# Linear attention and gated MLP on one core: another table of order, normalization as multiply-add, a tail by batch halves, more filler matmuls

## The chip, the core and the metric

The kernel runs on one core of a Trainium2 chip. The metric is the device time of one execution in microseconds (us). The engines are TensorE (PE, its weight loads PEld), VectorE (DVE), ScalarE (ACT), GpSimd (POOL) and SyncE (SP, which here only issues DMAs). Each engine takes its instructions strictly in the order in which the program lists them and waits on semaphores for the others.

## The reference

Linear attention with exponential features, then a feed-forward block with a spatial gate. B = 8 batches, H = 8 heads, S = 576 tokens, D = 64, F = 128, model width 512, inner width 1024.

```python
def phi(x):
    proj = np.einsum('bhsd,df->bhsf', x, w_phi)
    proj = proj - np.max(np.abs(proj), axis=-1, keepdims=True)
    return np.concatenate([np.exp(proj), np.exp(-proj)], axis=-1)
q_p, k_p = phi(q), phi(k)
kv = np.einsum('bhsf,bhsd->bhfd', k_p, v)
z = np.sum(k_p, axis=2)
num = np.einsum('bhsf,bhfd->bhsd', q_p, kv)
den = np.einsum('bhsf,bhf->bhs', q_p, z)[..., None] + 1e-06
x = (num / den)                       # then heads side by side: (B, S, 512)
h = np.maximum(x @ w_in, 0.0)
u, v = h[..., :512], h[..., 512:]
v_n = (v - mean(v)) / np.sqrt(var(v) + 1e-06)
v_s = np.einsum('ts,bsd->btd', w_spatial, v_n) + b_spatial[None, :, None]
out = (u * v_s) @ w_out
```

## The kernel before

**Tiling.** The 576 tokens of a batch are 512 in four chunks of 128, and a tail of 64. The tails of two batches make one tile of 128 rows; such a pair of batches is a group `g` (four groups). Most steps exist in a main form and in a form for tails, with a `t` in its name.

**The table of order.** The body of the kernel is a list of words, `ORDER`, which is read from left to right; each word calls one small function that issues the instructions of one step, and nothing reorders them. So the table sets the order on every engine and in every DMA queue. A word such as `qp.1.0.1:1,4` is the step `qp` for batch 1, half 0, head group 1, with its output in PSUM banks 1 and 4; `@A`, `@V`, `@P`, `@S` choose the engine where there is a choice; in other words the number behind the colon is a buffer of the step's kind of tile.

**The steps, keys.** `lk` loads a batch of k (POOL's queue, with a cast), `xk` turns it by a DMA transpose (SP's queue), `kp` projects it into two PSUM banks (8 matmuls, line 517), `km` takes the largest absolute value (VectorE, 522), `ke` makes the two exponentials (ScalarE, 526), `kem` those of the maxima, `vs` scales v by these on POOL (575), `kv` multiplies the two (606, 608), `kvc` copies the product out.

**Queries.** `lq`, `xq`, `qp`, `qm` correspond; `qs` splits the maxima into two bf16 parts (POOL, 623 and 624), `qt` transposes them, `qc` copies, `qf` makes the transposed projection less the maxima in two banks (633, 637), `qe` the exponentials (642), `qn` numerator and denominator (689), `qr` and `qx` the quotient (695, 702). `xx` turns the result by a DMA transpose, `tx` and `txc` do the same on TensorE.

**Feed-forward.** `vm` (798) and `um` (880) are the two halves of the first product, `vr` and `ur` their rectifiers, `vb` and `va` mean and variance, `vx` adds epsilon (VectorE, 803), `vw` takes the power -0.5 (POOL, 806), `vn` normalizes (POOL, 809), `sm` is the spatial product (895, 897), `sg` the gate (904), `om` the last product (909), `oc` its copy, `od` the store. `warm` issues matmuls of the identity into a bank that nobody reads. `lin`, `lout`, `lsp`, `lspt`, `lbs` load the weights, `spt`, `spc`, `spb` prepare the spatial ones.

**PSUM.** All eight banks are one tile of 128 x 8 x 512 f32. A step with one bank uses `bank(i)`; a step with two uses a slice with a step between its two banks:

```python
def pair(i, j):
    return ps[:, bass.ds(i, 2, step=j - i), :]
```

The waits between engines are put in when the program is built, from the tiles and slices that instructions read and write. Steps with two banks are `kp`, `km`, `ke`, `qp`, `qm`, `qf`, `qe`, `qn`, `qr`, `qx` and their tail forms.

Of the kernel before, what the change touches and what calls it, by code (L numbers as in the profile page):

```python
# [17 lines left out]
zvst.0@V lkf.0:0,0@S lkf.1:1@S lkf.2:2@S lq0.0.4:1 lkf.3:3@S lphi.0@A lphi.1@A lq0.4.4 lv.0.1:0@A zsp@V zmhl.0@V  # L18
lk.1:2 cident lv.0.0:1@A cphi@V zvnt.1@A ckf.1@A ckf.2@P lkt.0:0@S ckf.0@V warm.2:7 tk.0.0.0:0 csel tkc.0.0.0:0@V
warm.3:7 kp.0.0:1,2 tk.0.0.1:3 warm.10:7 tk.0.1.0:4 tkc.0.0.1@A chalf@P zmhl.1@V csel2@V km.0.0:0 ke.0.0.0:0 zmhl.2@V  # L20
ckf.3@P kem.0.0:0 kp.0.1:5,6 ke.0.0.1 lqt.0:1@S xq.0.0:1 lvt.0:0@S tkc.0.1.0:2@V xq.0.1:3 warm.3:3 kp.0.2:0,7 km.0.1:1
lv.2.0:2@S tk.0.1.1:3 ke.0.1.0:1 tkc.0.1.1@V km.0.2:2 ckt.0:0@P tkt.0:4 tktc.0:0@V kp.0.3:1,3 kem.0.1:1 kpt.0:2,4
ke.0.1.1 lq.1:0 vs.0.0.0:0@P km.0.3:3 kmt.0:0 qp.0.0.0:5,6 ke.0.2.0:2 ke.0.2.1 kemt.0:2 qm.0.0.0:0 qp.0.1.0:0,7
kem.0.3:3 qm.0.1.0:1 xk.1.0:4 ke.0.3.0:3 qs.0.0.0:0@V qp.0.0.1:5,6 lin.0 ket.0.0:0 ke.0.3.1 qs.0.1.0:1@V vs.0.0.1@P
vs.0.1.0:1@P qt.0.1.0:0 qt.0.0.0:7 cqt.0:0@V qp.0.1.1:1,3 qc.0.1.0:0@A qc.0.0.0:1@A qm.0.0.1:2 ket.0.1 vst.0.0.0:0@P
# [125 lines left out]
def kernel(  # L151
# [16 lines left out]
    nc = tc.nc  # L168
# [836 lines left out]
```

## Time and profile before

| | us |
|---|---|
| three timed runs | 452.3, 453.0, 456.23 (median 453.0) |
| the profiled execution | 445.4 |
| its span, first to last instruction | 443.6 |
| PE / PEld busy | 290.5 / 171.9 |
| DVE / ACT / POOL busy | 221.6 / 195.2 / 216.0 |
| mean granted TensorE clock | 0.807 |

Times in a profile are counted from the first instruction of the program. "Busy" is the time in which an engine had an instruction under way; of TensorE the ends are modelled, and the clock that was granted to it is shown beside. A group's row gives line, engine, operation, tiles and shapes, count, busy time and mean ns of one, then the idle time just before these instructions and what ended it. DMA moved 44.1 MB, at about 200 GB/s in the first 55 us and 99 GB/s over the span.

### The profile page before, as it was taken

What the parts mean: (1) busy time and instruction counts of PE and PEld (TensorE: products, weight loads), DVE (VectorE), ACT (ScalarE), POOL (GpSimd) and SP (SyncE); (2) the same over time, 40 slices, a digit from 0 to 9 for tenths busy, and PEclk for the clock granted to TensorE, in tenths of its full rate; (3) what the DMA queues carried; (4) which work ended last, traced back from release to release, by engine and by line L of the source; (5) the groups of instructions that cost most, each with busy time, mean ns of one, the idle gap of its engine ahead of it and who ended that gap; (6) DMA issues with size and microseconds to landing.
All of it is one profiled execution on the core that took longest, in us unless ns stands there. A gap on an engine that the chain in (4) does not pass through costs nothing. (4 is left out here: it accounts for less than half of the span.)

```text
span 443.6 us, 7949 instructions
## 1 busy us (share of the span) xinstructions
PE 290.5 (65%) x3184; PEld 171.9 (39%) x3184; DVE 221.6 (50%) x411; ACT 195.2 (44%) x314; POOL 216.0 (49%) x280
## 2 busy tenths in 40 slices
PE   4246463555765446554765668687879767699996
PEld 3125322224444233322333344344535535444452
DVE  5463424434853343332334358647778643666452
ACT  4254334344853433243242456375776555113032
POOL 3552241235674292501098029195579695446600
PEclk9556655666966766666677869999999999999999
DMA  8999965150980633936044748174233115012245
GB/s 198 203 225 222 191 121 99 20 72 0 148 151 2 143 49 47 193 46 142 1 62 82 110 69 160 33 190 113 33 84 72 51 24 120 2 25 83 60 142 191
DMA packets 91065, 44.11 MB, mean 99 GB/s; under 512 B 59986, under 2 KB 86290, under 8 KB 91028
## 3 DMA queue, kind: packets, MB, share of 16 engines
q1 hardware_dynamic: 72388, 32.39, 33.7%
q0 software_dynamic: 17424, 10.10, 17.7%
q10 hardware_dynamic: 1216, 1.11, 0.8%
q8 instruction: 25, 0.41, 0.4%
q14 instruction: 12, 0.10, 0.1%
HBM read 32.85 MB, written 9.44 MB: 95 GB/s over the span
## 5 line engine op out<-in xcount | busy, mean ns | idle before, releaser
L642 ACT ACTIVATE qf<-banks 128x1024 bf16<-128x1024 f32 x72 | 71.9, 1024 | 79.8 <-PE banks L880 11.9
L575 POOL TENSOR_TENSOR vs<-v,em 128x512 bf16<-128x512 f32 x62 | 64.1, 1041 | 87.5 <-ACT em L532 66.5
L526 ACT ACTIVATE kf<-banks 128x1024 bf16<-128x1024 f32 x64 | 65.1, 1027 | 64.6 <-DVE mk L522 20.4
L522 DVE TENSOR_REDUCE mq<-banks 128x8 f32<-128x1024 f32 x36 | 43.9, 1220 | 47.7 <-PE banks L608 9.6
L809 POOL TENSOR_SCALAR vn<-vr,mv,rs 128x512 bf16<-128x512 bf16 x30 | 62.1, 2073 | 1.1
L522 DVE TENSOR_REDUCE mk<-banks 128x8 f32<-128x1024 f32 x36 | 43.8, 1220 | 29.3 <-PE banks L608 9.4
L517 PE MATMUL banks<-wphi,T 64*128 64x128 bf16 x512 | 32.3, 262 | 37.6 <-ACT kf L526 11.2
L798 PE MATMUL banks<-w_in,xT 128*128 128x512 bf16 x128 | 40.0, 446 | 13.6 <-DVE x L702 4.2
L806 POOL TENSOR_TENSOR rs<-mv,neghalf 128x2 f32<-128x2 f32 (+1 forms) x20 | 13.7, 684 | 66.1 <-DVE mv L803 62.1
L895 PE MATMUL banks<-w_spT,vn 128*128 128x512 bf16 x128 | 36.3, 410 | 7.9 <-ACT kf L526 4.3
L517 PEld LDWEIGHTS <-T 64*128 64x128 bf16 x512 | 21.3, 112 | 51.8 <-issue 43.9
L606 PE MATMUL banks<-vs,kf 128*128 128x66 bf16 x512 | 30.4, 215 | 15.1 <-ACT qf L642 4.8
L880 PE MATMUL banks<-xT,w_in 128*128 128x512 bf16 x128 | 35.8, 415 | 2.4 <-ACT ob L253 1.5
L606 PEld LDWEIGHTS <-kf 128*128 128x128 bf16 x512 | 27.6, 112 | 23.0 <-issue 10.5
L909 PE MATMUL banks<-w_out,uT 128*128 128x512 bf16 x128 | 33.8, 401 | 3.4 <-DVE x L702 2.0
L689 PE MATMUL banks<-kv,qf 128*128 128x66 bf16 x512 | 25.6, 209 | 12.1 <-ACT qf L642 4.8
L689 PEld LDWEIGHTS <-qf 128*128 128x128 bf16 x512 | 23.7, 109 | 21.5 <-issue 17.8
L904 DVE TENSOR_TENSOR uT<-banks,uT 128x512 bf16<-128x512 f32 x32 | 21.5, 683 | 20.3 <-PE banks L897 11.5
L702 DVE TENSOR_TENSOR x<-banks,rc 128x512 bf16<-128x512 f32 x32 | 22.1, 690 | 17.3 <-PE banks L517 5.7
L253 ACT COPY ob<-banks 128x512 f32<-128x512 f32 x23 | 13.2, 587 | 38.5 <-PE banks L909 24.0
L608 PE MATMUL banks<-vst,kft 128*128 128x66 bf16 x128 | 25.4, 214 | 0.0
L798 PEld LDWEIGHTS <-xT 128*128 128x128 bf16 x128 | 12.7, 107 | 29.2 <-issue 19.6
(117 smaller groups left out, 466.5 us busy)
## 6 DMA issues: line engine op xcount, KB each, us to landing
out_dram<-ob SPq DMA_DIRECT2D x32, 256.0 KB, 2.7
v<-in_v_dram SPq DMA_DIRECT2D x14, 512.0 KB, 4.8
ld<-in_k_dram POOLq DMA_DIRECT2D x7, 512.0 KB, 7.9
ld<-in_q_dram POOLq DMA_DIRECT2D x7, 512.0 KB, 6.8
ob<-in_k_dram SPq DMA_DIRECT2D x4, 256.0 KB, 3.1
v<-in_v_dram ACTq DMA_DIRECT2D x2, 512.0 KB, 12.8
tf<-in_k_dram SPq DMA_DIRECT2D x8, 128.0 KB, 5.1
tf<-in_q_dram SPq DMA_DIRECT2D x8, 128.0 KB, 5.9
```

The costliest lines, as they stand in the source:

```text
L517: nc.tensor.matmul(out=bank(banks[y])[:, n * F:(n + 1) * F], lhsT=xT[halves[y], n, :], rhs=wphi[halves[y], :], start=True, stop=True)
L522: nc.vector.tensor_reduce(out=out_, in_=pp.rearrange("p y (n f) -> p y n f", f=F), axis=AX.X, op=ALU.max, apply_absolute_value=True)
L526: nc.scalar.activation(out=kf[:, s].rearrange("p y n f -> p y (n f)"), in_=pp, func=AF.Exp, bias=0.0, scale=(1.0, -1.0)[s])
L575: ENG[e].tensor_tensor(out=at["vs", (b, j)][:, s, :, 0:D], in0=at["v", (b, j // 2)][:, (j % 2) * n:(j % 2 + 1) * n, :], in1=at["em", (b, j ...
L606: nc.tensor.matmul(out=pv[:, hh, s, :], lhsT=kf[:, s, c % 2, 2 * hh + c // 2, :], rhs=w[:, s, NB * hh + c, :], start=(c == 0), stop=False)
L642: nc.scalar.activation(out=at["qf", u][:, s].rearrange("p y n t -> p y (n t)"), in_=at["pq", u], func=AF.Exp, bias=0.0, scale=(1.0, -1.0)[s])
L689: nc.tensor.matmul(out=at["pn", u][:, y, n, :], lhsT=f[:, s, y, n, :], rhs=at["kv", b][:, hg * HH + n, s, :], start=(s == 0), stop=(s == 1))
L798: nc.tensor.matmul(out=bank(place), lhsT=lhs[:, kc, :], rhs=w_in[:, kc, HALF:DFF], start=(kc == 0), stop=(kc == KC - 1))
L809: ENG[e].tensor_scalar(out=out_, in0=in_, scalar1=mv, scalar2=rs, op0=ALU.subtract, op1=ALU.mult)
L880: nc.tensor.matmul(out=bank(place).rearrange("p (c t) -> p c t", c=NB), lhsT=w_in[:, kc, dc * P:(dc + 1) * P], rhs=at["xT", b][:, :, kc, : ...
L895: nc.tensor.matmul(out=bank(place), lhsT=at["vn", b][:, c, cs], rhs=w_spT[:, c, 0:T0], start=(c == 0), stop=False)
L909: nc.tensor.matmul(out=bank(place), lhsT=at["uT", b][:, dc, c * P:(c + 1) * P], rhs=w_out[:, dc, :], start=(dc == 0), stop=(dc == KC - 1))
```

## The change

Nothing of the buffers changes. What changes:

- **Normalization.** `vn` and `vnt` compute x * rs + m rather than (x - mean) * rs. `vx` (now `prepare`) adds epsilon to the variance and negates the mean, in two instructions; the new steps `vy` and `vyt` multiply the negated mean by `rs` on POOL, behind `vw`.
- **Tails.** The steps behind a tail's features (`qnt` to `vnt`) take a part: 0 or 1 for one batch of the group, 2 for both. Group 0 is run in two parts, groups 1 to 3 whole. Group 0's parts are turned on TensorE (`txt`, `txtc`), group 3 as before, groups 1 and 2 by DMA as before.
- **Loads.** The loads of tails are written by one helper with the same two DMAs. `lphi` is one DMA on SP's queue rather than two on ACT's. `lk`, `lq` and `lv` are unchanged.
- **Fillers.** `warm` writes the last quarter of a bank. There are 117 of its matmuls in 12 words rather than 18 in four: 25, 10, 9, 12, 7, 5, 2, 20, 7, 12, 4 and 4, all ahead of `qt.0.1.0`.
- **The table.** All of `ORDER` is new: other places, other banks and buffers, and other engines for some copies and rectifiers (`vr` 23 on ACT and 9 on VectorE, before 14 and 18; `txc` 6 and 2, before 2 and 6). The feed-forward steps of batch 0 stand right behind its attention; `lsp`, `lspt`, `lin` and `lout` are issued earlier, `lq.1`, `lk.2`, `lq.2` later.

The first words of the old and of the new table, and the place in each where the feed-forward block of batch 0 begins:

```diff
-zvst.0@V lkf.0:0,0@S lkf.1:1@S lkf.2:2@S lq0.0.4:1 lkf.3:3@S lphi.0@A lphi.1@A lq0.4.4 lv.0.1:0@A zsp@V zmhl.0@V
-lk.1:2 cident lv.0.0:1@A cphi@V zvnt.1@A ckf.1@A ckf.2@P lkt.0:0@S ckf.0@V warm.2:7 tk.0.0.0:0 csel tkc.0.0.0:0@V
...
-qr.0.1.1:0 txc.0.1@V kem.1.1:1 qp.1.0.0:2,5 ke.1.0.1 ke.1.1.0:0 kem.1.0:3 kp.1.2:0,7 lbs:0@S qx.0.1.1 qtt.0:1 vm.0.0:3
-qm.1.0.0:1 qp.1.1.0:2,5 vs.1.1.0:0@P vst.0.1.1@P qct.0:0@V vm.0.1:1 km.1.2:3 ke.1.1.1 vr.0.0:0@A ke.1.2.0:1 tx.0.2:4
...
+zsp@V zmhl.1@V zmhl.0@V zmhl.2@V cident lkf.0:0,0@S csel zvnt.1@A lkf.2:1@S zvnt.0@A lphi@S ckf.0@V warm.25:0
+tk.0.0.0:0 lkf.1:2@S lkt.0:0@S lkf.3:3@S lq0.0.4:1 ckf.2@V tkc.0.0.0:0@A warm.10:0 tk.0.1.0:1 lv.0.0:0@A cphi@V
...
+vbt.0.0:0 qr.0.1.1:1 txc.0.1@V vat.0.0:0 vst.0.1.1@P vm.0.0:4 vxt.0.0 qx.0.1.1 spc.4@A vm.0.1:6 vr.0.0:1@V ckt.1:0@P
+lv.1.1:3@S tx.0.2:3 vwt.0.0:0 vb.0.0:1 tx.0.3:2 lq.2:1 vr.0.1:2@A spt.3:0 kp.1.0:1,7 kp.1.1:4,5 txc.0.3@A vyt.0.0
...
```

The functions:

```diff
...
         return bass.AP(tensor=t.tensor, offset=t.offset + (b * H + h0) * S * D,
                        ap=[[NB * D, P], [S * D, n], [1, NB * D]])
 
-    def tail_ap(t, b):
-        return bass.AP(tensor=t.tensor, offset=t.offset + b * H * S * D + T0 * D,
-                       ap=[[D, TL], [S * D, H], [1, D]])
-
-    rows = [slice(0, TL), slice(TL, 2 * TL)]
+    def load_tail(e, out_, t, g):
+        for bl in range(2):
+            ENG[e].dma_start(out=out_[bl * TL:(bl + 1) * TL],
+                             in_=bass.AP(tensor=t.tensor, offset=t.offset + (2 * g + bl) * H * S * D + T0 * D,
+                                         ap=[[D, TL], [S * D, H], [1, D]]))
+
+    rows = [slice(0, TL), slice(TL, 2 * TL), slice(0, P)]
+    parts = [(0,), (1,), (0, 1)]
     halves = [slice(0, D), slice(D, P)]
     ops = {}
 
...
         make_identity(nc, ident)
 
     @op
-    def lphi(e, i):
-        ENG[e].dma_start(out=wphi_f[i * D:(i + 1) * D, :], in_=w_phi)
+    def lphi(e):
+        ENG[e].dma_start(out=wphi_f, in_=bass.AP(tensor=w_phi.tensor, offset=w_phi.offset, ap=[[0, 2], [F, D], [1, F]]))
 
     @op
     def cphi(e):
...
     @op
     def warm(e, n, place):
         for i in range(n):
-            nc.tensor.matmul(out=bank(place)[:, 0:F], lhsT=ident, rhs=ident, start=True, stop=True)
+            nc.tensor.matmul(out=bank(place)[:, 3 * P:4 * P], lhsT=ident, rhs=ident, start=True, stop=True)
 
 
 
...
 
     @op
     def lkt(e, g, place):
-        t = take("tf", ("k", g), place)
-        for i in range(2):
-            ENG[e].dma_start(out=t[rows[i]], in_=tail_ap(k, 2 * g + i))
+        load_tail(e, take("tf", ("k", g), place), k, g)
 
     @op
     def lqt(e, g, place):
-        t = take("tf", ("q", g), place)
-        for i in range(2):
-            ENG[e].dma_start(out=t[rows[i]], in_=tail_ap(q, 2 * g + i))
+        load_tail(e, take("tf", ("q", g), place), q, g)
 
     @op
     def ckt(e, g, place):
...
 
     @op
     def lvt(e, g, place):
-        t = take("vt", g, place)
-        for i in range(2):
-            ENG[e].dma_start(out=t[rows[i]], in_=tail_ap(v, 2 * g + i))
+        load_tail(e, take("vt", g, place), v, g)
 
     @op
     def lin(e, i):
...
         query_exp(g, s)
 
     @op
-    def qnt(e, g, p0, p1):
-        at["pn", g] = sums((p0, p1))
+    def qnt(e, g, i, p0, p1):
+        at["pn", g, i] = sums((p0, p1))
         for y in range(2):
             for n in range(HH):
                 for s in range(2):
-                    for bl in range(2):
+                    for bl in parts[i]:
                         r = rows[bl]
-                        nc.tensor.matmul(out=at["pn", g][r, y, n, :], lhsT=at["qf", g][:, s, y, n, r],
+                        nc.tensor.matmul(out=at["pn", g, i][r, y, n, :], lhsT=at["qf", g][:, s, y, n, r],
                                          rhs=at["kv", 2 * g + bl][:, 2 * n + y, s, :], start=(s == 0), stop=(s == 1))
 
     @op
-    def qrt(e, g, place):
-        nc.vector.reciprocal(out=take("rc", g, place), in_=at["pn", g][:, :, :, D:D + 1])
-
-    @op
-    def qxt(e, g, place):
-        nc.vector.tensor_tensor(out=take("xt", g, place).rearrange("p (n y) d -> p y n d", y=2),
-                                in0=at["pn", g][:, :, :, 0:D], in1=at["rc", g].to_broadcast([P, 2, HH, D]),
-                                op=ALU.mult)
+    def qrt(e, g, i, place):
+        nc.vector.reciprocal(out=take("rc", (g, i), place)[rows[i]], in_=at["pn", g, i][rows[i], :, :, D:D + 1])
+
+    @op
+    def qxt(e, g, i, place=None):
+        if place is not None:
+            take("xt", g, place)
+        r = rows[i]
+        nc.vector.tensor_tensor(out=at["xt", g].rearrange("p (n y) d -> p y n d", y=2)[r],
+                                in0=at["pn", g, i][r, :, :, 0:D],
+                                in1=at["rc", (g, i)][r].to_broadcast([r.stop - r.start, 2, HH, D]), op=ALU.mult)
 
 
 
...
         nc.sync.dma_start_transpose(out=take("xTt", g, place), in_=at["xt", g].rearrange("p h d -> p (h d)"))
 
     @op
-    def txt(e, g, place):
+    def txt(e, g, i, place):
         pt = bank_bf(place)[:, 0:KC * P].rearrange("p (n t) -> p n t", t=P)
+        r = rows[i]
         for kc in range(KC):
-            nc.tensor.transpose(out=pt[:, kc, :], in_=at["xt", g][:, 2 * kc:2 * kc + 2, :], identity=ident)
-        at["px", g] = pt
-
-    @op
-    def txtc(e, g, place):
-        copy(e, take("xTt", g, place), at["px", g])
-
-
-
-    def v_mm(lhs, place):
+            nc.tensor.transpose(out=pt[:, kc, r], in_=at["xt", g][r, 2 * kc:2 * kc + 2, :], identity=ident[r, r])
+        at["px", g, i] = pt[:, :, r]
+
+    @op
+    def txtc(e, g, i, place=None):
+        if place is not None:
+            take("xTt", g, place)
+        copy(e, at["xTt", g][:, :, rows[i]], at["px", g, i])
+
+
+
+    def v_mm(lhs, place, r=slice(0, P)):
         for kc in range(KC):
-            nc.tensor.matmul(out=bank(place), lhsT=lhs[:, kc, :], rhs=w_in[:, kc, HALF:DFF], start=(kc == 0),
+            nc.tensor.matmul(out=bank(place)[r], lhsT=lhs[:, kc, r], rhs=w_in[:, kc, HALF:DFF], start=(kc == 0),
                              stop=(kc == KC - 1))
-        return bank(place)
-
-    def add_eps(mv):
-        nc.vector.tensor_scalar(out=mv, in0=mv, scalar1=1e-6, scalar2=None, op0=ALU.add)
-
-    def root(rs, mv):
-        nc.gpsimd.tensor_tensor(out=rs, in0=mv, in1=neghalf[:, 0:rs.shape[1]], op=ALU.pow)
+        return bank(place)[r]
+
+    def prepare(mv):
+        nc.vector.tensor_scalar(out=mv[:, :, 1], in0=mv[:, :, 1], scalar1=1e-6, scalar2=None, op0=ALU.add)
+        nc.vector.tensor_scalar(out=mv[:, :, 0], in0=mv[:, :, 0], scalar1=-1.0, scalar2=None, op0=ALU.mult)
+
+    def root(rs, mv, r=slice(0, P)):
+        nc.gpsimd.tensor_tensor(out=rs, in0=mv, in1=neghalf[r, 0:rs.shape[1]], op=ALU.pow)
+
+    def shift(mv, rs):
+        nc.gpsimd.tensor_tensor(out=mv, in0=mv, in1=rs, op=ALU.mult)
 
     def normalize(e, out_, in_, mv, rs):
-        ENG[e].tensor_scalar(out=out_, in0=in_, scalar1=mv, scalar2=rs, op0=ALU.subtract, op1=ALU.mult)
+        ENG[e].tensor_scalar(out=out_, in0=in_, scalar1=rs, scalar2=mv, op0=ALU.mult, op1=ALU.add)
 
     @op
     def vm(e, b, c, place):
...
 
     @op
     def vx(e, b, cc):
-        add_eps(at["mv", (b, cc)][:, :, 1])
+        prepare(at["mv", (b, cc)])
 
     @op
     def vw(e, b, cc, place):
         root(take("rs", (b, cc), place).rearrange("p n o -> p (n o)"), at["mv", (b, cc)][:, :, 1])
+
+    @op
+    def vy(e, b, cc):
+        shift(at["mv", (b, cc)][:, :, 0], at["rs", (b, cc)][:, :, 0])
 
     @op
     def vn(e, b, c, place=None):
...
         normalize(e, at["vn", b][:, c, 0:HALF], at["vr", (b, c)], at["mv", (b, cc)][:, y, 0:1], at["rs", (b, cc)][:, y, :])
 
     @op
-    def vmt(e, g, place):
-        at["pV", g] = v_mm(at["xTt", g], place)
-
-    @op
-    def vrt(e, g, place):
-        relu(e, take("vr", g, place), at["pV", g])
-
-    @op
-    def vbt(e, g, place):
-        nc.vector.bn_stats(out=take("st", g, place), in_=at["vr", g])
-
-    @op
-    def vat(e, g, place):
-        nc.vector.bn_aggr(out=take("mv", g, place)[:, 0, :], in_=at["st", g])
-
-    @op
-    def vxt(e, g):
-        add_eps(at["mv", g][:, 0, 1:2])
-
-    @op
-    def vwt(e, g, place):
-        root(take("rs", g, place)[:, 0, :], at["mv", g][:, 0, 1:2])
-
-    @op
-    def vnt(e, g, place):
-        t = take("vnt", g, place)
-        for bl in range(2):
+    def vmt(e, g, i, place):
+        at["pV", g, i] = v_mm(at["xTt", g], place, rows[i])
+
+    @op
+    def vrt(e, g, i, place):
+        relu(e, take("vr", (g, i), place)[rows[i]], at["pV", g, i])
+
+    @op
+    def vbt(e, g, i, place):
+        nc.vector.bn_stats(out=take("st", (g, i), place)[rows[i]], in_=at["vr", (g, i)][rows[i]])
+
+    @op
+    def vat(e, g, i, place):
+        nc.vector.bn_aggr(out=take("mv", (g, i), place)[rows[i], 0, :], in_=at["st", (g, i)][rows[i]])
+
+    @op
+    def vxt(e, g, i):
+        prepare(at["mv", (g, i)][rows[i], 0:1, :])
+
+    @op
+    def vwt(e, g, i, place):
+        root(take("rs", (g, i), place)[rows[i], 0, :], at["mv", (g, i)][rows[i], 0, 1:2], rows[i])
+
+    @op
+    def vyt(e, g, i):
+        shift(at["mv", (g, i)][rows[i], 0, 0:1], at["rs", (g, i)][rows[i], 0, :])
+
+    @op
+    def vnt(e, g, i, place=None):
+        if place is not None:
+            take("vnt", g, place)
+        for bl in parts[i]:
             r = rows[bl]
-            normalize(e, t[r, bl, :], at["vr", g][r], at["mv", g][r, 0, 0:1], at["rs", g][r, 0, :])
+            normalize(e, at["vnt", g][r, bl, :], at["vr", (g, i)][r], at["mv", (g, i)][r, 0, 0:1],
+                      at["rs", (g, i)][r, 0, :])
 
 
 
```

## The prediction

> **What bounds the kernel now.** I read the page first, then the stretches between chosen points of the order of work, then the instructions in order of time, then the groups.
>
> ```profile
> span 443.6 us, 7949 instructions
> ...
> PE 290.5 (65%) x3184; PEld 171.9 (39%) x3184; DVE 221.6 (50%) x411; ACT 195.2 (44%) x314; POOL 216.0 (49%) x280
> ...
> PEclk9556655666966766666677869999999999999999
> ```
>
> No engine is busy for more than 65% of the span, so no engine bounds it as a whole. TensorE's granted clock is 0.5 to 0.8 of full speed in nearly all of the first 24 of 40 slices (some 266 us) and full afterwards. Priced at full clock (0.86 us for four matmuls of 512 columns, 0.43 us for eight of 128, 0.5 us for sixteen of 66, all from late rows of the chain) TensorE's work is 245 us. I cut the order into stages of 12 us of such work and timed each by its first matmul. In the rows below the columns are the stretch, its length, busy time of PE, PEld, DVE, ACT and POOL, granted clock, DMA share and GB/s.
>
> ```profile
> 83.10:114.20 31.10, 17.12 (x185) 10.44 (x186) 14.82 (x22) 15.29 (x30) 12.12 (x22) 0.70 0.28 32
> 114.20:139.70 25.50, 14.81 (x247) 10.98 (x247) 15.49 (x31) 16.04 (x23) 14.34 (x22) 0.79 0.86 122
> ...
> 235.20:263.80 28.60, 17.65 (x155) 9.93 (x155) 12.40 (x22) 11.56 (x18) 10.61 (x18) 0.73 0.66 101
> ...
> 277.40:294.00 16.60, 12.15 (x133) 6.42 (x129) 9.70 (x19) 9.54 (x18) 7.21 (x13) 1.00 0.49 116
> ...
> 367.70:386.10 18.40, 12.25 (x218) 8.47 (x215) 8.31 (x23) 6.41 (x11) 7.34 (x6) 1.00 0.33 70
> ```
>
> The third and the fourth row hold nearly the same work, yet take 28.6 and 16.6 us. DMA is nearly idle in the first row, so after the first 50 us loads are not the reason. The reason shows in time order (start, length, engine, instruction, idle time and what ended it):
>
> ```profile
> 60.68 1.92 PE L798 MATMUL banks<-w_in,xT 128*128 128x512 bf16 x4
> ...
> 62.70 1.23 DVE L522 TENSOR_REDUCE mq<-banks 128x8 f32<-128x1024 f32 x1 [2.13 <-PE banks L798]
> ...
> 63.98 0.61 PE L517 MATMUL banks<-wphi,T 64*128 64x128 bf16 x8 [1.38 <-DVE mq L522]
> ...
> 66.45 1.22 DVE L522 TENSOR_REDUCE mk<-banks 128x8 f32<-128x1024 f32 x1 [2.39 <-PE banks L798]
> ...
> 67.71 1.02 ACT L526 ACTIVATE kf<-banks 128x1024 bf16<-128x1024 f32 x1 [6.76 <-DVE mk L522]
> ```
>
> The maximum at 62.70 reads PSUM banks 2 and 5. Its own matmuls were done, but it waits for `vm.0.0`, which writes bank 3. The one at 66.45 reads banks 0 and 7 and waits for `vm.0.1` in bank 1. A pair with a gap is guarded as the whole stretch between its ends. I call such a wait a crossing: a wait among TensorE, VectorE and ScalarE whose two instructions share no bank. Counted in the built programs, the 21 stages of before have 18, 36, 16, 19, 32, 27, 29, 26, 8, 12, 20, 6, 10, 10, 14, 21, 0, 1, 2, 4, 1. The stages of 26 to 32 crossings (numbers 4 to 7, from 0) take 34.6, 31.6, 29.3 and 28.6 us, mean 31.0; those of 12 to 21 after the clock has risen 16.6, 16.3, 16.0 and 18.4, mean 16.8; those of 6 to 10 13.6, 13.3, 12.5 and 15.6, mean 13.8; those of 0 to 4 about 12. (Stages 0 to 3 also carry the start, or 15 to 18 us of VectorE and ScalarE work each: 38.6, 40.0, 31.1, 25.5.) So where crossings are dense the engines take turns, TensorE goes idle, and its clock follows:
>
> ```profile
> 81.10:84.51 3.41, 3.41 (x29) 1.96 (x24) 1.72 (x3) 0.64 (x1) 0.25 (x2) 0.50 0.00 0
> 84.51:87.93 3.42, 0.69 (x11) 0.23 (x8) 1.57 (x2) 1.02 (x1) 0.00 (x0) 1.00 0.00 0
> 87.93:91.34 3.41, 0.61 (x8) 0.38 (x8) 0.88 (x2) 2.59 (x5) 1.81 (x3) 0.50 0.00 0
> ...
> 285.90:289.31 3.41, 1.80 (x23) 1.04 (x20) 2.88 (x4) 1.57 (x6) 0.80 (x1) 1.00 0.72 138
> ```
>
> A full window of 3.41 us is followed by full clock, one at 20% by half; 53% (the last row) keeps it. The kernel thus has two self-holding states, and leaves the slow one at 262 us.
>
> The Trainium skill ("TensorE: Matmul & The Clock Gate", Part 1: The HAM clock gate) says that the array runs at half clock by default, that a busy window of about 3.4 us frees it and an idle one takes it back, and that the ramp costs under 1% of a typical span. The window agrees. The price does not: the mean granted clock here is 0.807, and a window need not be idle to lose it. By that rule the fillers would hold the clock from the start; the second rival below works that out from rows.
>
> **The change, part by part.**
>
> ```profile
> L575 POOL TENSOR_TENSOR vs<-v,em 128x512 bf16<-128x512 f32 x62 | 64.1, 1041 | 87.5 <-ACT em L532 66.5 <-issue 9.8 <-PE banks L517 8.2
> ...
> L809 POOL TENSOR_SCALAR vn<-vr,mv,rs 128x512 bf16<-128x512 bf16 x30 | 62.1, 2073 | 1.1
> ...
> L806 POOL TENSOR_TENSOR rs<-mv,neghalf 128x2 f32<-128x2 f32 (+1 forms) x20 | 13.7, 684 | 66.1 <-DVE mv L803 62.1 <-DVE mv L827 3.7
> ...
> L624 POOL TENSOR_TENSOR mhl<-mq,mhl 128x8 bf16<-128x8 f32 x33 | 6.7, 203 | 2.7
> ```
>
> *Multiply-add.* No row has multiply-then-add on POOL. Upper bound: the present 2073 ns. Lower bound: POOL's plain cast of a 128x512 tile, 618 ns. I take 1041 ns, the two-input multiply: it moves more data than the normalization, so the extra 1032 ns look like arithmetic. POOL has 30 + 8 normalizations now and 29 + 8 after: 78.7 us become 38.5 (22.9 to 76.7). Added: 21 small products `vy`, `vyt` at 203 ns (a tiny POOL product; at most 684 ns, the power), 4.3 us; on VectorE the preparation is two instructions in each of 21 places rather than one in 20, 22 x 216 ns = 4.8 us. `vy` waits for the power before it in the same queue; behind it stand the normalization and the next `vs`, held for its 0.2 us. POOL's sum falls by 36 us. Since POOL is busy 49% of the span and its waits end with others, I put 0 on the path. A batch's chain of four normalizations before `sm` shortens by 4 x 1.03 - 0.4 = 3.7 us, so the bounds are 8 x 3.7 = 30 us gained and, at an unchanged 2073 ns, 8 x 0.4 = 3 us lost.
>
> *Tail of group 0 by halves.* One more set of small steps: VectorE 0.2 (`qrt`) + 0.69 (`qxt`) + 0.66 (`vbt`) + 0.17 + 0.43 + up to 0.68 (`vrt`), 2.8 us; TensorE four more matmuls of 512 columns, 0.86 us, and eight transposes, 0.43 us; two 0.42 us copies for one DMA transpose that leaves SP's queue. All of it lies in the first 140 us, where every engine is at 25 to 65%: 0 on the path, 5 us at most.
>
> *Loads.* `lk`, `lq` of batches 1 to 7 already take whole batches and `load_tail` issues the same two DMAs: the diff does not make loads larger. In POOL's queue `lsp`, `lspt`, `lin.0` and `lout` (0.5 to 0.9 us of issue each) move ahead, `lq.1`, `lk.2` and `lq.2` back. Before `vm.0.0` the changed order needs k, q and v of batch 0 (1.05 MB each), three tails (0.26 each), w_spatial (1.33), k of batch 1 and half of w_in (1.05 each): 7.4 MB, at the measured 215 GB/s 34 us, hidden since that point comes near 62 us.
>
> *Fillers.* 117 instead of 18, at 0.11 us each at half clock: 11 us more of PE. Of the first 30 us PE is busy 9.5, so 20 us of gap cover them. The second run of them waits for a copy of ScalarE, and two transposes (`tk.0.1.0`) and all key matmuls queue behind it on TensorE. Uncovered they cost up to 11 us; I put 1.5.
>
> *The table.* This decides. The same engines carry nearly the same sums (VectorE's and ScalarE's move by 6 us or less), but the feed-forward half of batch 0 now stands right behind its attention, and crossings in the changed program, by stages of 12 us again, are 17, 33, 13, 15, 43, 4, 9, 6, 25, 8, 18, 21, 19, 26, 13, 7, 31, 18, 16, 4, 2. In all 348 against 312, but no longer packed into the first half. Priced by the rates above:
> - Stage 0 ends at `qp.0.0.1`, now begun at 28.5; with 1.5 for fillers 30. Stage 1 has the work that now lies between 28.5 and 57.6, plus two scaled exponentials and features of the tail, 4: 33, so 63.
> - Stage 2 like the 25.5 row: 25. Stage 3 has little VectorE and ScalarE work, between 16.8 and 25.5: 21. Stage 4 (43 crossings): 36. Together 145.
> - Stages 5 to 7: 16 while the clock returns, 2 x 13.8: 43.6. Sum 189.
> - Stage 8 (25), between the 18.4 of 21 crossings and the 28.6 of 26: 24. Stage 9: 15. Stages 10 to 12: 16.8 + 18.4 + 16.8 = 52. Stage 13 (26): 24. Stage 14: 16.8. Stage 15: 13.8. Sum 334.
> - Stage 16 (31): 31. Stages 17 and 18: 33.6, and 2 for the clock's return. Stages 19 and 20: 12 and 10.5. Sum 423.
> - The end: before's last 4.9 us of PE work took 9.8 us, so 5 more: **428 us of span**, against 443.6, a gain of 15.6 us.
>
> The profiled execution has 445.4 us, 1.8 beside its span, and the timed runs a median of 453.0, 7.6 above it. Of the unpriced shortening of the normalization chain (0 to 30) I take 7, which cancels that offset: **428 us** for the timed runs, 5.5% under 453.0.
>
> **Rivals.**
> *Slower: the crossings take the second half's clock.* Before runs 149 us of PE work after 264 us in 180 us because few crossings interrupt it. The changed table has 18 to 21 in stages 10, 11, 12 and 17. If a stage from 18 on cannot hold half-busy windows, these four cost 31.0 each instead of 17.2 (+55), and 8 and 13 31 instead of 24 (+14): 428 + 69 = 497 us. For it: all before's stages above 25 are slow. Against: 20 and 21 crossings went at full clock in 16.3 and 18.4 us. Deciding point: half clock in more than two stages behind the eighth.
>
> *Faster: the clock holds from the first stretch.* With fillers and TensorE-heavy stages from number 2 on, stages 2, 3, 4 at 16.8, 14, 25 (-26), 8 and 13 at 19 (-10), 16 at 20 (-11), stage 1 at 26 (-7): 374 us. Against: 33 and 43 crossings in stages 1 and 4.
>
> *The multiply-add is no cheaper on POOL.* Then POOL holds 22, 20 and 18 us in stages 2, 10 and 15; they become 25, 20 and 18 at least: +7, and the 7 are not gained: 442 us.
> The Trainium skill ("GPSIMD Engine Reference", 3.1 Elementwise) says that a body of up to two operations runs at 1.03 cycles an element, which would make 512 elements 0.44 us (an estimate from that page) in either form. The 2073 ns do not agree for the present form; no row shows the other.
>
> *Near no change.* Early gain and late loss cancel when stages 8, 13, 16 and one more are cold: 428 + 7 + 7 + 14 = 456.
>
> **How the numbers follow.** Forecast case (400 to 447, with the unchanged-multiply case in it) 0.46; clock held 0.14; near none 0.10; slower 0.30. Hence faster by over 1% (about what a measurement of this kernel can tell) 0.60, within 1% 0.10, slower 0.30. The range leaves out the best end of the held clock and the worst of the slow case: 385 to 485.
>
> **What would show it.** Right: full clock from about 150 us, half clock again only around stages 8, 13, 16 (some 200, 285, 345 us); VectorE maxima that wait for PE lines of other banks; `vm.0.0` near 63 us; `vn` near 1.04 us. Wrong: half clock throughout the second half, `vn` at 2.07 us, or full clock before 100 us.

## The result, and the profile after

| | us |
|---|---|
| changed kernel, timed runs | median 454.4 (451.2 to 460.0) |
| kernel before, timed beside it | median 452.0 (445.1 to 457.4) |
| ratio changed to before | 1.014, interval 1.011 to 1.018 |
| profiled execution, its span | 454.7, 452.6 (before 445.4, 443.6) |

The ratio compares the fast runs of either kernel alone; the kernel before has more slow ones, which is why the medians stand closer together than 1.4%. The forecast was 428 us, a gain of 5.5%: the change made the kernel 1.4% slower, not faster.

The page of the changed kernel (span; busy time of each engine; granted clock in tenths over 40 slices, with no clock on record for the first 44 us):

```profile
span 452.6 us, 8213 instructions
...
PE 309.3 (68%) x3295; PEld 181.9 (40%) x3295; DVE 222.9 (49%) x433; ACT 205.0 (45%) x327; POOL 167.5 (37%) x296
...
PEclk9999765958755579898869989679589997599999
```

POOL lost 48 us of work, and the span grew by 9. The clock is no longer low in one block of 24 slices and full behind it; it comes back near 160 us and is lost again and again until 400 us. By stages of 12 us of TensorE work (columns: stretch, length, PE, PEld, DVE, ACT and POOL busy, granted clock, DMA share, GB/s), these are numbers 4, 5, 12, 15 and 16:

```profile
121.20:160.60 39.40, 21.24 (x182) 12.10 (x182) 15.85 (x25) 16.34 (x25) 10.87 (x18) 0.50 0.55 120
160.60:174.70 14.10, 12.88 (x190) 7.81 (x190) 8.65 (x23) 10.07 (x17) 8.40 (x18) 0.88 0.01 1
...
285.90:309.10 23.20, 16.49 (x184) 9.58 (x183) 8.98 (x17) 8.76 (x15) 6.68 (x16) 0.76 0.29 74
...
354.30:366.10 11.80, 10.84 (x150) 6.33 (x150) 8.41 (x15) 8.00 (x12) 10.61 (x20) 1.00 0.22 68
366.10:389.80 23.70, 16.48 (x202) 9.99 (x202) 12.38 (x22) 10.63 (x19) 3.27 (x6) 0.77 0.24 68
```

Stage 4 with 43 crossings takes 39.4 us, stage 5 with 4 takes 14.1. The first eight stages end at 202.3 us (before 263.8), the rest takes 250.3 us (before 179.8): 61 us won early, 70 lost late. A crossing of stage 4, in time order:

```profile
159.37 1.21 DVE L524 TENSOR_REDUCE mq<-banks 128x8 f32<-128x1024 f32 x1
...
160.64 2.72 PE L806 MATMUL banks<-w_in,xT 128*128 128x512 bf16 x6 [2.51 <-DVE mq L524]
```

The matmul is `vm.1.2` into bank 2. TensorE is idle for 2.51 us until a maximum has read banks 1 and 5.

### The profile page after: what moved, and what is told of

Its sections match the earlier page's. It is cut to its first block, busy times and chain, and to the rows that moved or that the text cites. A ratio compares the mean times of both kernels' runs of the same rounds, so it can differ in the third digit from the quotient of the medians.

```text
span 452.6 us, 8213 instructions
## 1 busy us (share of the span) xinstructions
PE 309.3 (68%) x3295; PEld 181.9 (40%) x3295; DVE 222.9 (49%) x433; ACT 205.0 (45%) x327; POOL 167.5 (37%) x296
## 5 line engine op out<-in xcount | busy, mean ns | idle before, releaser
L644 ACT ACTIVATE qf<-banks 128x1024 bf16<-128x1024 f32 x72 | 72.3, 1027 | 78.7 <-DVE mq L524 12.7
L577 POOL TENSOR_TENSOR vs<-v,em 128x512 bf16<-128x512 f32 x64 | 66.3, 1042 | 76.4 <-ACT em L534 58.6
L524 DVE TENSOR_REDUCE mq<-banks 128x8 f32<-128x1024 f32 x36 | 43.6, 1220 | 37.2 <-PE banks L519 6.7
L519 PE MATMUL banks<-wphi,T 64*128 64x128 bf16 x512 | 31.4, 251 | 36.2 <-DVE x L704 14.9
L815 POOL TENSOR_TENSOR rs<-mv,neghalf 128x2 f32<-128x2 f32 (+2 forms) x21 | 14.0, 668 | 102.6 <-DVE mv L812 87.0
L806 PE MATMUL banks<-w_in,xT 128*128 128x512 bf16 x128 | 42.5, 473 | 6.3 <-DVE mq L524 2.7
L931 PE MATMUL banks<-w_out,uT 128*128 128x512 bf16 x128 | 37.8, 435 | 5.4 <-DVE mq L524 4.2
L926 DVE TENSOR_TENSOR uT<-banks,uT 128x512 bf16<-128x512 f32 x32 | 21.7, 685 | 25.1 <-PE banks L919 16.5
L691 PE MATMUL banks<-kv,qf 128*128 128x66 bf16 x512 | 26.7, 215 | 8.0 <-ACT qf L644 5.4
L691 PEld LDWEIGHTS <-qf 128*128 128x128 bf16 x512 | 24.5, 113 | 14.7 <-issue 12.4
L608 PE MATMUL banks<-vs,kf 128*128 128x66 bf16 x512 | 25.9, 202 | 2.9 <-ACT qf L644 1.8
L608 PEld LDWEIGHTS <-kf 128*128 128x128 bf16 x512 | 24.0, 103 | 9.5 <-issue 4.4
L625 POOL CAST mhl<-mq 128x8 bf16<-128x8 f32 x32 | 6.1, 191 | 57.1 <-DVE mq L524 56.9
L833 DVE BATCH_NORM_STATS2 st<-vr 128x6 f32<-128x512 bf16 x32 | 21.4, 684 | 5.9 <-ACT vr L264 5.7
L917 PEld LDWEIGHTS <-vn 128*128 128x128 bf16 x128 | 12.8, 106 | 27.6 <-issue 16.5
L697 DVE RECIPROCAL rc<-banks 128x8 f32<-128x8 f32 x32 | 6.5, 203 | 34.9 <-ACT qf L644 11.7
```

The costliest lines, as they stand in the source:

```text
L519: nc.tensor.matmul(out=bank(banks[y])[:, n * F:(n + 1) * F], lhsT=xT[halves[y], n, :], rhs=wphi[halves[y], :], start=True, stop=True)
L524: nc.vector.tensor_reduce(out=out_, in_=pp.rearrange("p y (n f) -> p y n f", f=F), axis=AX.X, op=ALU.max, apply_absolute_value=True)
L577: ENG[e].tensor_tensor(out=at["vs", (b, j)][:, s, :, 0:D], in0=at["v", (b, j // 2)][:, (j % 2) * n:(j % 2 + 1) * n, :], in1=at["em", (b, j ...
L608: nc.tensor.matmul(out=pv[:, hh, s, :], lhsT=kf[:, s, c % 2, 2 * hh + c // 2, :], rhs=w[:, s, NB * hh + c, :], start=(c == 0), stop=False)
L644: nc.scalar.activation(out=at["qf", u][:, s].rearrange("p y n t -> p y (n t)"), in_=at["pq", u], func=AF.Exp, bias=0.0, scale=(1.0, -1.0)[s])
L691: nc.tensor.matmul(out=at["pn", u][:, y, n, :], lhsT=f[:, s, y, n, :], rhs=at["kv", b][:, hg * HH + n, s, :], start=(s == 0), stop=(s == 1))
```

## The experiments

### Nearly all crossings taken out, and what the rest of the change is then worth

The banks behind the words were chosen anew so that the two banks of a pair are neighbours; word order, engines and buffers stay. Of the changed kernel (`e1_after_rebanked`) and of the kernel before (`e2_before_rebanked`), a sample each:

```diff
-kp.2.3:4,6 ... qp.2.1.1:1,5 ... vm.1.2:2 vm.1.3:3
+kp.2.3:6,7 ... qp.2.1.1:4,5 ... vm.1.2:0 vm.1.3:2
...
-kp.0.0:1,2 ... kp.0.2:0,7
+kp.0.0:4,5 ... kp.0.2:6,7
```

> The changed kernel with the same words in the same order on the same engines; only the PSUM banks behind the words differ: 144 of its 145 pairs are now neighbours (before this edit 36), chosen so that steps alive at the same time do not span one another. Counted in the built program, crossings fall from 348 to 21, and waits between instructions that do share a bank rise from 466 to 781. Theory (crossings make the engines take turns and that costs TensorE its clock): the clock is full from about 70 us on, every 12 us stage takes 12 to 16 us as the stages with 0 to 10 crossings did, stage 0 keeps about 40 us (fillers and late loads): 335 to 385 us, ratio to the kernel before 0.74 to 0.85. Rival (the order of the words and the mix of engines set the pace, crossings only show it): 440 to 455 us, and the same stages stay slow. Second rival (crossings cost, but the reuse of banks takes their place): between, 400 to 435 us.

> The kernel before with the same words, order and engines, only the PSUM banks chosen anew (141 of 144 pairs neighbours, before this edit 56): crossings 312 to 36, waits between instructions that share a bank 506 to 760. Theory: the slow first half goes (stages 4 to 7 took 31 us each with 26 to 32 crossings), stages 4 on take 12 to 17 us: 345 to 395 us. Since both tables then have almost no crossings, the difference that is left between this kernel and the re-banked changed one is that of the tables, the normalization and the start: the changed one should be slower in the first 45 us by about 10 us (28.5 to 40.9 at the same step) and win some of it back by the shorter normalization. Rival (order and engine mix): 440 to 453 us.

Measured: 291.7 us (291.2 to 293.0), ratio to before 0.655 (0.651 to 0.660); and 316.8 us (312.1 to 320.0), ratio 0.704 (0.693 to 0.716). Both are better than the theory's ranges. The page of the re-banked changed kernel, its stages 4 and 16, and the two instructions shown above:

```profile
span 289.4 us, 8198 instructions
...
PE 248.6 (86%) x3261; PEld 155.4 (54%) x3295; DVE 220.5 (76%) x433; ACT 200.6 (69%) x327; POOL 166.8 (58%) x296
...
PEclk9557799999979999999999999999999999999999
```

```profile
71.90:88.80 16.90, 13.74 (x186) 8.29 (x184) 14.16 (x25) 14.86 (x25) 9.99 (x18) 0.90 1.00 162
...
225.50:238.20 12.70, 11.97 (x199) 8.14 (x201) 10.23 (x19) 9.11 (x18) 1.68 (x2) 1.00 0.44 106
```

```profile
88.37 1.90 PE L805 MATMUL banks<-w_in,xT 128*128 128x512 bf16 x7
...
89.40 1.21 DVE L523 TENSOR_REDUCE mq<-banks 128x8 f32<-128x1024 f32 x1
```

The same words in the same order need 39.4 and 23.7 us with crossings, 16.9 and 12.7 without. The matmuls of `vm.1.2` and `vm.1.3` now begin with no wait, 1.0 us ahead of the maximum that `vm.1.2` used to wait for. VectorE, ScalarE and POOL do the same work; TensorE does its own in 61 us less busy time at a higher clock, and the other 102 us of span are idle time that went. The rival (order and mix of engines set the pace) falls.

### Only the names of the banks changed

Re-banking also changes which step reuses a bank. So the eight banks of the changed kernel were renamed by a fixed permutation, once for fewer crossings (first new lines) and once for more (second):

```diff
-kp.2.3:4,6 ... qp.2.1.1:1,5 ... vm.1.2:2 vm.1.3:3
+kp.2.3:0,6 ... qp.2.1.1:1,4 ... vm.1.2:2 vm.1.3:5
...
+kp.2.3:0,2 ... qp.2.1.1:5,6 ... vm.1.2:1 vm.1.3:3
```

> The changed kernel with its eight banks only renamed by one fixed permutation (0 to 7 become 3, 4, 2, 5, 6, 1, 0, 7): which steps follow one another in a bank is exactly as in the changed kernel, but the stretches between the two banks of a pair cover others. Crossings 348 to 290. The two re-banked kernels lost 0.50 us for each crossing taken away ((454.4 - 291.7) / 327) and 0.49 us ((453 - 316.8) / 276). Theory (crossings alone): 454 - 58 x 0.5 = 425 us, 410 to 440; the gain in the stages that lose most (8, from 25 to 10; 11, from 21 to 8; 16, from 31 to 12). Rival (neighbouring pairs or a better order of reuse made the re-banked kernels fast): within 1% of the changed kernel, 450 to 458 us.

> The changed kernel with its banks renamed by another fixed permutation (0 to 7 become 4, 5, 1, 3, 0, 6, 2, 7): crossings 348 to 403, reuse of banks as in the changed kernel. Theory: 454 + 55 x 0.5 = 482 us, 465 to 500; stages 5 to 7 (4, 9, 6 crossings, now 19, 25, 19) go from 12 to 16 us to 20 to 30. Rival (reuse or neighbours): within 1% of the changed kernel.

Measured: 424.2 us (421.5 to 427.1) and 501.6 us (500.6 to 504.6). The first is as expected, the second 20 us more than the linear price. Stages 15 and 16 with fewer, then with more crossings:

```profile
339.40:349.90 10.50, 10.45 (x148) 6.26 (x149) 7.99 (x13) 7.91 (x12) 9.25 (x18) 1.00 0.25 76
...
349.90:364.90 15.00, 12.26 (x203) 8.27 (x203) 12.14 (x22) 10.91 (x20) 3.48 (x5) 1.00 0.38 108
```

```profile
376.10:399.00 22.90, 13.95 (x148) 7.98 (x149) 9.80 (x18) 9.05 (x12) 10.66 (x20) 0.85 0.11 35
...
399.00:430.00 31.00, 17.36 (x198) 10.77 (x201) 8.68 (x16) 9.78 (x17) 3.19 (x4) 0.72 0.18 52
```

Stage 15 has 1, 7 and 19 crossings in the three namings and takes 10.5, 11.8 and 22.9 us; stage 16 has 12, 31 and 35 and takes 15.0, 23.7 and 31.0. All stages, each with its crossings and us (stage 0 from the span's start to the word `qp.0.0.1`; some stages are joined, since 34 matmul records are missing in each of the last three traces, where a border is good to 0.8 us):

| stage | forecast | changed | fewer | more | re-banked |
|---|---|---|---|---|---|
| 0 | 17: 30 | 40.9 | 27: 47.4 | 26: 44.4 | 3: 32.0 |
| 1 | 33: 33 | 30.7 | 26: 24.5 | 26: 26.0 | 1: 14.1 |
| 2 | 13: 25 | 29.1 | 12: 23.7 | 11: 20.1 | 0: 13.7 |
| 3 | 15: 21 | 20.5 | 16: 19.8 | 20: 21.5 | 2: 12.1 |
| 4 | 43: 36 | 39.4 | 37: 40.3 | 38: 32.5 | 0: 16.9 |
| 5 to 7 | 19: 43.6 | 41.7 | 36: 59.8 | 63: 77.1 | 1: 37.6 |
| 8 | 25: 24 | 25.7 | 10: 14.4 | 31: 27.6 | 0: 12.1 |
| 9 | 8: 15 | 17.8 | 13: 17.2 | 17: 21.3 | 0: 12.2 |
| 10 | 18: 16.8 | 17.6 | 15: 18.7 | 8: 14.3 | 0: 11.4 |
| 11, 12 | 40: 35.2 | 45.7 | 22: 37.2 | 40: 54.2 | 3: 26.7 |
| 13 | 26: 24 | 26.8 | 18: 17.7 | 18: 24.3 | 0: 10.3 |
| 14 | 13: 16.8 | 18.4 | 15: 18.7 | 5: 12.8 | 0: 12.7 |
| 15 | 7: 13.8 | 11.8 | 1: 10.5 | 19: 22.9 | 0: 13.8 |
| 16 | 31: 31 | 23.7 | 12: 15.0 | 35: 31.0 | 1: 12.7 |
| 17, 18 | 34: 35.6 | 34.5 | 24: 30.9 | 40: 40.2 | 4: 22.6 |
| 19 to end | 6: 27.5 | 28.3 | 6: 28.7 | 6: 28.3 | 6: 28.6 |

Fitted through zero, the two renamings change a stage by 0.71 us for each crossing more or less (correlation 0.91 over 32 differences). So crossings cause the time; the reuse of banks, which a renaming keeps, does not. The number of neighbouring pairs moved along with the crossings (36 of 145 pairs in the changed kernel, 54 with fewer crossings, 31 with more), so these two runs alone do not part the two. But an instruction on neighbouring banks is no faster. The maxima of the changed kernel, and of the re-banked one, where 144 of 145 pairs are neighbours:

```profile
L524 DVE TENSOR_REDUCE mq<-banks 128x8 f32<-128x1024 f32 x36 | 43.6, 1220 | 37.2 <-PE banks L519 6.7
```

```profile
L523 DVE TENSOR_REDUCE mq<-banks 128x8 f32<-128x1024 f32 x36 | 43.2, 1216 | 8.2 <-PE banks L518 7.1
```

One takes 1220 and 1216 ns; what falls is the idle time before them, from 37.2 to 8.2 us.

### The multiply-add, four times

Changed kernel with the old normalization, with crossings (`e4_subtract_multiply`) and re-banked (`e7_rebanked_subtract`); kernel before with the multiply-add, with crossings (`e9_before_multiply_add`) and re-banked (`e10_before_rebanked_multiply_add`). The first pair's edit; the second pair's is its reverse, with the product issued right behind the power:

```diff
     def prepare(mv):
...
-        nc.vector.tensor_scalar(out=mv[:, :, 0], in0=mv[:, :, 0], scalar1=-1.0, scalar2=None, op0=ALU.mult)
...
     def shift(mv, rs):
-        nc.gpsimd.tensor_tensor(out=mv, in0=mv, in1=rs, op=ALU.mult)
+        pass
...
-        ENG[e].tensor_scalar(out=out_, in0=in_, scalar1=rs, scalar2=mv, op0=ALU.mult, op1=ALU.add)
+        ENG[e].tensor_scalar(out=out_, in0=in_, scalar1=mv, scalar2=rs, op0=ALU.subtract, op1=ALU.mult)
```

> The changed kernel with the old normalization: (x - mean) * rs in one instruction, no negation of the mean and no product vy. The table is the same (vy does nothing). Theory (prediction: POOL's normalization is mostly covered): the instruction takes 2.07 us again on POOL instead of 0.775, POOL's sum rises by 37 x 1.3 - 4 = 44 us to about 212, and the total rises by 2 to 12 us, mostly in the late stages where the four normalizations of a batch stand ahead of the spatial product (8 batches x 4 x 1.3 = 41 us at most, if none were covered). Rival (normalization on the path of every batch): 30 to 41 us longer, 482 to 494 us. Second rival (it is wholly covered): within 2 us of the changed kernel.

> The re-banked changed kernel (21 crossings) with the old normalization, (x - mean) * rs in one instruction, without the negation and the product vy. With crossings this edit cost 14 us (468.0 against 454.4). Theory: with TensorE busy for 86% of the span the normalization is still largely covered, but the four of a batch ahead of the spatial product are not all; 6 to 20 us more than 291.7, so 298 to 312 us. That would be a good part of the 25 us by which the re-banked changed kernel beats the re-banked kernel before (291.7 against 316.8). Rival (TensorE hides it): within 3 us of 291.7, and the 25 us come from the table and the start alone.

> The kernel before with the multiply-add alone: the negated mean in a second VectorE instruction, the product behind the power on POOL, the normalization as x * rs + m. Table and banks as before, 312 crossings. The prediction put 0 on the path from POOL's smaller sum and took 7 us from the shorter chain (30 us gained to 3 lost). In the changed table the same exchange was worth 13.6 us (468.0 against 454.4), without crossings 32.9 us (324.6 against 291.7). Theory (crossings hide most of it, because the engines take turns and POOL's work lies beside): 438 to 448 us, 5 to 15 us gained. Rival (as in the re-banked kernel, POOL decides): 420 to 425 us.

> The re-banked kernel before (316.8 us, 36 crossings) with the multiply-add. Its chain had 14% on POOL, of it 8% or 25 us in the normalization line. Theory (the normalization is on the path once crossings are gone): 285 to 300 us, about what the re-banked changed kernel takes (291.7), so that the table, the tails by halves, the fillers and the loads are together worth nothing to a few us either way. Rival (the new table is what made the re-banked changed kernel faster): 308 to 317 us.

| table | banks | subtract, multiply | multiply, add |
|---|---|---|---|
| changed | as changed | 468.0, ratio 1.047 (1.038 to 1.055) | 454.4, ratio 1.014 (1.011 to 1.018) |
| changed | re-banked | 324.6 (322.9 to 326.5) | 291.7, ratio 0.655 (0.651 to 0.660) |
| before | as before | 452.0 to 454.6 | 452.3, ratio 1.004 (1.000 to 1.009) |
| before | re-banked | 316.8, ratio 0.704 (0.693 to 0.716) | 312.7, ratio 0.693 (0.685 to 0.700) |

In the old table it is worth nothing that can be measured, in the new one 14 us with crossings and 33 without. All four expectations missed: 2 to 12 us, 6 to 20, 5 to 15 and 17 to 32 were expected, in the order of the texts above, and 14, 33, none and 4 came, the 4 with ratios that overlap. The instruction on POOL in the changed kernel and in its re-banked form with the old one, and the latter's chain of waits:

```profile
L821 POOL TENSOR_SCALAR vn<-vr,rs,mv 128x512 bf16<-128x512 bf16 x29 | 22.4, 775 | 1.0
```

```profile
L820 POOL TENSOR_SCALAR vn<-vr,mv,rs 128x512 bf16<-128x512 bf16 x29 | 60.2, 2079 | 0.8
```

```profile
PE 38%; POOL 27%; DVE 14%; DMA 9%; issue 5%; ACT 5%; SPq 1%; POOLq 0%; DVEq 0%; ACTq 0%
POOL vn L820 17%; PE banks L916 8%; DVE mq L523 5%; PE banks L930 5%; DMA tf<-in_k_dram 4%; POOL vnt L820 4%; PE banks L607 4%; PE banks L690 3%; PE banks L518 3%; PE banks L805 3%; POOL rs L814 3%; DMA xT<-x 2%; PE banks L918 2%; DVE mk L523 2%; PE banks L634 2%
```

With the slow instruction POOL holds 27% of the chain; in the re-banked changed kernel it holds 2%. Of the 35 us by which this kernel's span is longer, 32 lie in six places: stages 2, 6 with 7, 9, 10, 14 and 19 take 4.6, 5.2, 6.8, 4.5, 4.0 and 6.8 us more. What sets the tables apart shows in the row of the spatial product `sm`, which reads the normalized tile. With the old instruction, it is for the re-banked changed table, the re-banked old table, and the changed table with crossings:

```profile
L916 PE MATMUL banks<-w_spT,vn 128*128 128x512 bf16 x121 | 38.8, 431 | 23.2 <-POOL vn L820 21.5
```

```profile
L895 PE MATMUL banks<-w_spT,vn 128*128 128x512 bf16 x120 | 33.0, 389 | 1.9 <-DVE uT L904 0.7
```

```profile
L917 PE MATMUL banks<-w_spT,vn 128*128 128x512 bf16 x121 | 38.2, 432 | 19.2 <-POOL vn L821 9.2
```

In the changed table TensorE waits for normalizations, 21.5 us without crossings and 9.2 us with them; in the old table no `sm` waits for one, with crossings or without. So the changed table puts the normalizations of a batch closer ahead of its spatial products than the old one does, and only there does a shorter instruction come through to TensorE; no run moved those words alone. The 8% that `vn` held of the chain of the re-banked old table was no measure of its worth: 4 us came of 25. What the four cells do show is that table and multiply-add belong together: without crossings the rest of the change loses 8 us (316.8 to 324.6), and with the multiply-add in both it wins 21 (312.7 to 291.7).

### Fillers

The last six of the twelve filler words left out, 49 of 117 matmuls, with crossings and re-banked:

```diff
-... ke.0.2.1 warm.2:4 tqt.0:4 ... ke.0.1.0:2 warm.20:4 qpt.0:4,5 ... ke.0.3.1 warm.7:1
+... ke.0.2.1 tqt.0:4 ... ke.0.1.0:2 qpt.0:4,5 ... ke.0.3.1
...
-kem.0.3:0 warm.12:2 qft.0:1,3 ... qs.0.1.0:1@V warm.4:2 qp.0.0.1:2,6 ... qet.0.0:0 warm.4:0 qt.0.1.0:0
+kem.0.3:0 qft.0:1,3 ... qs.0.1.0:1@V qp.0.0.1:2,6 ... qet.0.0:0 qt.0.1.0:0
```

> The changed kernel without the last six filler words (2, 20, 7, 12, 4, 4 matmuls: 49 of 117), nothing else. Theory: these 49 stand on TensorE's path between 28 and 42 us and cost about 5 us there (49 at 0.11 us at half clock), and they do not raise the clock: the first queries begin about 5 us earlier than 40.95, and the total is 3 to 7 us shorter than the changed kernel, about the time of the kernel before. Rival (fillers pay by the clock): without them stage 1 runs at a lower clock and the total is the same or up to 10 us longer. The counted crossings change by stage only by the shift of the stage borders.

> The re-banked changed kernel without its last six filler words (49 of 117 matmuls). There the 20 fillers stand at 21.4 us while TensorE waits for ScalarE until 23.4 anyway, and the clock is granted in full from some 32 us. Theory (they cost the path 2 to 3 us where nothing covers them: the 7 at 27.3, the 12 at 29.1): 288 to 292 us. Rival (they bring the clock up earlier, now that no crossing takes it away again): without them the first queries run at half clock and the full clock comes some 10 to 20 us later: 295 to 303 us.

Measured: 451.1 us, ratio 1.012 (1.003 to 1.021), 3 us less by the medians, but by its interval not to be told from the changed kernel's 1.014; and 293.7 us (291.8 to 294.7) against 291.7, between what the two theories gave. With crossings `qp.0.0.1` begins at 36.1 us instead of 40.9, as expected, and `vm.0.0` at 66.6 instead of 71.6; how much of it reaches the end stays open. Without crossings the kernel is 2 us slower by the medians when the 49 are gone, but the ranges overlap: that fillers win anything is not shown. The Trainium skill ("TensorE: Matmul & The Clock Gate", Part 1: The HAM clock gate) lets a busy window free the clock. Here the real work does that too once crossings do not stop it: over four executions each, the mean granted clock is 0.956 to 0.967 with all fillers and 0.938 to 0.953 without the 49, against 0.784 to 0.857 over the executions of the changed kernel with all of them.

### The first loads

```diff
-cident lkf.0:0,0@S csel zvnt.1@A lkf.2:1@S zvnt.0@A lphi@S ckf.0@V warm.25:0 tk.0.0.0:0 lkf.1:2@S lkt.0:0@S lkf.3:3@S
+cident lkf.0:0,0@S lphi@A csel zvnt.1@A lkf.2:1@S zvnt.0@A lkf.1:2@S lkf.3:3@S ckf.0@V warm.25:0 tk.0.0.0:0 lkt.0:0@S
...
-csel2@V lspt:4 warm.9:0 ... tk.0.0.1:6 lsp:0 ckt.0:0@P ... tqtc.0:0@V lin.0
+csel2@V warm.9:0 ... tk.0.0.1:6 ckt.0:0@P ... tqtc.0:0@V lspt:4 lsp:0 lin.0
```

> The changed kernel with another order of its first loads, nothing else: the load of w_phi goes first on ACT's queue instead of third on SP's, the four parts of k of batch 0 go ahead of the tails on SP, and the two loads of w_spatial (1.33 MB) move behind the first queries on POOL's queue. In the changed kernel w_phi landed at 10.2 us, the last part of k at 17.5. Theory (the start was mis-sized by the loads): the first projection begins at 7 to 8 us instead of 10.5, `qp.0.0.1` at 32 to 37 instead of 40.95, the total 4 to 8 us below 454.4. Rival (crossings swallow it, as with the fillers, where the same step came 4.8 us earlier and the total fell by 3 us at most): within 3 us of 454.4.

> The re-banked changed kernel (291.7 us) with the same new order of the first loads. There the chain waits for the last part of k from 4.4 to 17.5 us, and `qp.0.0.1` begins at 32.0. Theory (without crossings a start that is earlier by some us is kept to the end): 281 to 287 us. Rival (the DMA engines are busy for 0.8 to 0.9 of the first 70 us, so that what is moved forward is paid by w_spatial and the later batches): 289 to 294 us.

What it undoes, in the changed kernel (SPq is the issue of a DMA on SP's queue):

```profile
4.87 5.88 SPq L345 DMA_DIRECT2D ob<-in_k_dram  x1
...
10.21 0.23 DVE L260 CAST wphi<-wphi_f 128x128 bf16<-128x128 f32 x1 [5.60 <-DMA wphi_f<-in_w_phi_dram]
...
10.49 0.61 PE L519 MATMUL banks<-wphi,T 64*128 64x128 bf16 x8 [3.52 <-DVE wphi L260]
...
17.66 0.60 POOL L260 CAST tl<-tf 128x512 bf16<-128x512 f32 x1 [13.38 <-DMA tf<-in_k_dram]
```

POOL waits 13.38 us for the first tail, w_phi keeps VectorE waiting for 5.60 us and with it the first projection, and the last part of k needs 5.88 us to be issued alone. Measured: 448.9 us, ratio 0.999 (0.994 to 1.004), and 288.2 us, ratio 0.638 (0.630 to 0.646). The first projection begins at 7.5 us instead of 10.5, `qp.0.0.1` at 36.2, `vm.0.0` at 66.0 instead of 71.6, and the gain of 5 to 6 us is kept. Re-banked, `qp.0.0.1` moves from 32.0 to 28.2 and 3.5 us are kept, between the theory's 5 to 10 and the rival's nothing; the ranges (286.4 to 290.9 against 291.2 to 293.0) just part. 288.2 us is the fastest version of all, 36% under the kernel before.

## Why the prediction was wrong

**The reading of the bound was right.** Crossings set the pace and the clock follows them: fewer, more and nearly none of them, with all words kept, gave 424, 502 and 292 us.

**The sum of stages failed by two terms.** The forecast's stages add up to 428 us and the span was 452.6. Of the 24 us:
- *Stage 0, "30", measured 40.9.* This step failed first. The 28.5 of before was taken over with 1.5 for fillers, although the changed table has 17 crossings up to `qp.0.0.1` and the old one 9. The three things left unpriced were each taken away alone: crossings (32.0, so 8.9 us), the new load order (36.2, 4.7 us) and the last fillers (36.1, 4.8 us, of which 0.6 stand there before the first filler left out). They overlap, or go beyond what the change put in, as 18.4 us are more than the 12.4 by which the step came later than in the kernel before. Without crossings the step begins at 32.0 us in the changed table and at 30.7 in the old one, which had begun it at 28.5 with its 9: there they cost nothing that shows. The changed table also has four words for the queries' tail (`tqt.0`, `qpt.0`, `qtt.0`, `qft.0`) ahead of this step, and the old one behind it; no run moved them. The loads were called "hidden since that point comes near 62 us"; this looked at the amount of bytes before `vm.0.0`, not at which load the first projection waits for.
- *Stages 11 and 12, "18.4 + 16.8", measured 45.7.* They were priced from before's stages with 12 to 21 crossings, all at full clock; the two took 22.5 and 23.2 us. Stage 11 nearly kept the clock (0.94), but has 12.8 us of VectorE work and 11.5 of ScalarE, where before's row of 18.4 us has 8.3 and 6.4. I read this as engines that take turns adding up their work, so that one crossing costs more where more work stands behind it; no run varied that work alone. (The two rows of before that the forecast called nearly the same work differ in it too: 12.4 and 11.6 us in the longer, 9.7 and 9.5 in the shorter.) Stage 12 has 9.0 and 8.8 us of such work, little more than that row, but ran at a clock of 0.76, with TensorE busy for 16.5 us instead of some 12. That 19 crossings would leave the clock full, as 20 and 21 had done before, was the wrong step there; why the clock went stays open.
- *Stages 2, 4, 9 and 13* were 2.8 to 4.1 us longer each, 13 together; stages 1, 5 to 7, 15 and 16 were 14 us shorter, of it 7.3 in stage 16. One price by the number of crossings thus did not hold from stage to stage: the two renamings gave 0.52 and 0.86 us for one.

**The term of the normalization failed, both ways.** The size of the instruction was put at 1041 ns and measured 775, inside its bounds. Its worth on the path was put at 0 from POOL's smaller sum and 7 us from the shorter chain; it was nothing in the old table and 14 us in the new one, where TensorE waits for it. With the old instruction the changed kernel is 4.7% slower than the kernel before, and the multiply-add gives 3.3% of it back. The 7 us had been set against 7.6 us between profile and median; the changed kernel's median does not stand above its profiled execution (454.4 and 454.7), so this offset was none.

**Of the rivals**, the one called near no change came closest: 456 us against 454.4. Its shape was right (early gain, late loss), its places were not, so the near hit is luck: it has stages 8, 13 and 16 at 31 us, they took 25.7, 26.8 and 23.7, and the loss lay in stages 0, 11 and 12. The slower rival's deciding point, half clock in more than two stages behind the eighth, was met in part: six of the stages from 9 to 18 ran at 0.75 to 0.90, none at half throughout. That half clock would come again "only around stages 8, 13, 16" was wrong, and `vm.0.0` came at 71.6 us, not near 63.

**Tails by halves** were never run alone. What is left of the change after the multiply-add, the fillers and the loads is the table with them in it.

## What to carry to other kernels

Ask of each wait whether its two instructions touch the same memory: a strided slice that is guarded as one whole stretch gave waits that cost about 0.5 us each, and choosing neighbouring banks for the same words took 30% off one kernel and 36% off the other. A schedule's worth cannot be told while such waits are in it: the changed kernel loses 1.4% with them and wins 25 us without (316.8 to 291.7). Price a stage by rows with the same engines' work, and price the first stage like every other. A share of the chain of waits is no price: 8% of it, 25 us, gave 4.

## What the runs showed of the hardware

- On POOL (x - mean) * rs took 2073 to 2079 ns for 128x512 bf16, x * rs + m 766 to 775 ns. The Trainium skill ("GPSIMD Engine Reference", 3.1 Elementwise) gives bodies of up to two operations one rate of 1.03 cycles an element; the two forms differ by a factor of 2.7 here. On VectorE they do not differ: in the old table both took 406 ns, two instructions each.
- The price of a crossing is not constant. The 58 taken out by renaming were worth 30 us (0.52 each), the 55 put in cost 47 us (0.86 each).
- A load of one part of k took 5.88 us of SP's queue to issue behind six others, against 0.97 us for the first two parts together.
